# Hashed attention and Fourier mixing: the reciprocals of a head pair copied in two parts, and sums of weight quarters placed behind the newest mask or tally

## The chip, the cores and the metric

The kernel runs on one core of one Trainium2 chip. The metric is device time in microseconds (us), the median of several executions; before the change it is 1086.68 us (three runs, 1086.46 to 1087.05). The core has five engines that work side by side and wait for each other by semaphores: TensorE (PE, with its weight loads listed as PEld), VectorE (DVE), ScalarE (ACT), GpSimd (POOL) and SyncE (SP), which here only issues transfers.

## The reference

Two blocks follow each other. The first is attention over 4 batches of 8 heads, 768 positions and 64 numbers a head, in which a query sees only keys that fall in the same hash bucket:

```python
q_bits = (np.einsum('bhsd,dk->bhsk', q, proj) > 0).astype(np.int64)   # 6 bits; k likewise
mask = q_bucket[:, :, :, None] == k_bucket[:, :, None, :]
scores = scale * np.matmul(q, k.transpose(0, 1, 3, 2))
scores = np.where(mask, scores, -1000000000.0)
...
attn = attn / (np.sum(attn, axis=-1, keepdims=True) + 1e-09)
return np.matmul(attn, v).astype(np.float32)
```

The heads laid side by side make x (4 x 768 x 512). The second block mixes x by a Fourier transform and puts a normalised two-layer network behind it:

```python
mixed = np.real(np.fft.fft(np.fft.fft(x, axis=1), axis=2))
u = x + mixed
un = (u - mu) / np.sqrt(var + 1e-06)
ch = np.maximum(un @ w_ch1, 0.0) @ w_ch2      # 512 -> 2048 -> 512
return (u + ch).astype(np.float32)
```

## The kernel before, in words

**Pairs and chunks.** Two heads make a pair, so each batch has four pairs, n = 0 to 15 in all. A pair's 768 keys are taken in six chunks c of 128. For a chunk, `scores` (L884) multiplies keys and queries on PE into two banks (matmul `sc`, L905, one bank for each half of the queries); `weights` (L914) takes the exponential on ACT into a buffer `pk` (L916), of which there are two in turn; from pair 5 on, `weigh` (L920) multiplies by the mask of equal buckets on DVE (L930, one instruction per head); `chunk` adds the result to a running tally `acc` on DVE (L1018), which becomes the denominator; and `values` (L936) multiplies by the values on PE (`oo`, L941). Because there are two `pk` buffers, the exponential of chunk c waits for the values and the tally of chunk c-2.

**The end of a pair.** `scale` (L947) is a generator, run in two steps. The first step moves the result to x on ACT, adds up the tally over the keys on PE (`sum`, L960), transposes the sums on DVE (L967) and takes reciprocals (L969, L970). The second step copies the reciprocals into place with eight small copies on ACT (L976, 32 x 12 numbers each), spreads them by a transpose on DVE (L977) and multiplies x by them (L981). The second step is called from the chunk loop of the next pair, at the next visit of that loop after the first step; `finish` (L987) does the first.

**Preparing a pair.** While pair n runs, `prepare` (L766) gets pair n+1 ready: the transposes of q and k on DVE (L779), the signs of the projections (matmul `bits`, L836; test on DVE, L840) and the bucket numbers (matmuls `qb` L850 and `kb` L860, moved out of the banks by copies or casts on DVE and ACT, L535 and L537).

**Mixing.** `fold` (L1083) and the rest of `mix` (L1116) make the Fourier transform: sums and differences on DVE, matmuls `cs` (L1133) and `A`, `B` (L1162), added to x on DVE (L1176). Then `mlp7` (L1383) does the network by a scheme of seven products in place of eight. Its first layer, `inner` (L1448), has products `h_p` (L1441) and their sums on ACT and DVE (L1463 to L1492); the second, `outer7` (L1295), has products `o` (L1320), each scaled and added to the result on DVE (L1332 and others) with some copied on ACT first (L1339, L1350, L1353). Banks for `sum`, `bits`, `cs`, `A`, `B`, `h_p`, `o` all come from one pool of two (`pt`, tiles of the pool `ps_1`); scores have their own two and values their own two.

**Weights.** During the mix of batch 0 the second layer's weights are converted from the form in which they arrive, and `weights2` (L1260) forms four sums of their quarters on DVE (L1286 to L1289), once for every two pieces converted, eight times in all.

**Order.** Batch 0's attention is under a hand-written order. From batch 1 on, the generator of the mix of batch b-1 is advanced inside the chunk loop of attention b, and a scheduler decides the order of each engine's queue from the order of the program, the dependencies and its own durations, with two helpers on top. `behind` (L877) ties an instruction to the newest scores or values matmul and raises its priority. `in_turn` (L684) ties what stands in it to the newest instructions on record in a table `done_by`, one for each engine; exponentials, masks, some copies and additions of the first layer and of the Fourier step enter themselves there:

```python
    def in_turn():
        with ExitStack() as st:
            for ins in done_by.values():
                st.enter_context(tc.issue_after(ins.ins))
            yield
```

Of the kernel before, what the change touches and what calls it, by code (L numbers as in the profile page):

```python
# [17 lines left out]
ALU = mybir.AluOpType  # L18
# [8 lines left out]
NPAIR = H // 2  # L27
# [458 lines left out]
def _main(  # L486
# [13 lines left out]
    nc = tc.nc  # L500
# [13 lines left out]
    def wt(shape, dtype, tag, name, bufs=2):  # L514
        return work.tile(shape, dtype, tag=tag, name=name, bufs=bufs)
# [4 lines left out]
    def pt(shape, name):  # L520

        turn[0] += 1
        if roomy[0] and turn[0] % 2:
            if turn[0] % 4 == 1:
                return ps_o.tile(shape, F32, tag="o", name=name)
            return ps_sc.tile(shape, F32, tag="sc", name=name)
        return ps_1.tile(shape, F32, tag="ps", name=name)
# [152 lines left out]
    ET = mybir.EngineType  # L680
    done_by = {}

    @contextmanager
# [6 lines that stand above are left out]
# [186 lines left out]
    @contextmanager  # L876
    def behind():  # L877

        with tc.issue_after(last[0].ins), tc.high_priority(offset=AHEAD):
            yield  # L880
# [55 lines left out]
    def values(n, c, pk, oos):  # L936

        for g in range(2):
            w = HALF + 1 - g
            for h in range(2):  # L940
                oo = nc.tensor.matmul(  # L941
                    oos[g][h * D : (h + 1) * D, 0:w], nat["v", n][:, (2 * c + h) * D : (2 * c + h + 1) * D],
                    pk[:, g, h, 0:w], start=(c == 0), stop=(c == NT - 1),
                )
        last[0] = oo

    def scale(n, oos, sums):  # L947


        x = xs[n // NPAIR][:, n % NPAIR]  # L950
        vs = wt([P, 1], F32, "vs", f"vs{n}")
        nc.scalar.copy(vs, oos[0][:, HALF : HALF + 1])
        halves = [x[:, g * HALF : (g + 1) * HALF] for g in range(2)]
        for g, xg in enumerate(halves):
            nc.scalar.activation(xg, oos[g][:, 0:HALF], AF.Identity, bias=vs)

        ps = pt([P, HALF], f"sum{n}")
        for i, part in enumerate(sums):
            for j in range(4):
                nc.tensor.matmul(  # L960
                    ps[32 * j : 32 * j + 32, :], ones, part[:, j // 2, j % 2],
                    start=(i == 0), stop=(i == len(sums) - 1),
                )


        rt = wt([P, S], F32, "rt", f"rt{n}", 1)
        nc.vector.transpose(rt[:, 0:HALF], ps)  # L967
        rc = wt([P, HALF // 32], F32, "rc", f"rc{n}")
        nc.vector.tensor_scalar(rc, rt[:, 0:HALF:32], S * EPS, None, op0=ALU.add)  # L969
        nc.vector.reciprocal(rc, rc)  # L970
        yield
        rr = wt([P, 2, HALF // 32], F32, "rr", f"rr{n}")
        for g in range(2):
            for i in range(4):
                j = 2 * g + i // 2
                nc.scalar.copy(rr[32 * i : 32 * i + 32, g], rc[32 * j : 32 * j + 32])  # L976
        nc.vector.transpose(  # L977
            rt.rearrange("p (j i) -> p j i", i=32),
            rr.rearrange("p g j -> p (g j)")[:, :, None].broadcast_to([P, S // 32, 32]),
        )  # L980
        nc.vector.tensor_tensor(x, x, rt, op=ALU.mult)  # L981

    def attention(b):
        xs[b] = wt([P, NPAIR, S], F32, "x", f"x{b}")
        pending, scales = [], []

        def finish():  # L987
            n, c, pk, oos, sums = pending.pop(0)
            with behind() if n >= NPAIR and t is not None else nullcontext():
                values(n, c, pk, oos)  # L990
            if c == NT - 1:
                scales.append(scale(n, oos, sums))
                next(scales[-1])

        for t in range(NPAIR):
            n = NPAIR * b + t
            half = fold(b, 0) if t == NPAIR - 1 else iter(())
            if 1 < n + 1 < NPAIR * B:
                load(n + 1)
            ahead = prepare(n + 1) if n + 1 < NPAIR * B else iter(())  # L1000
            oos = [ps_o.tile([P, 512], F32, tag="o", name=f"oo{n}_{g}") for g in range(2)]
            acc = wt([P, 2, 2, HALF], F32, "acc", f"acc{n}", 1)
            first = None
            def chunk(c, pss):

                nonlocal first
                pk = weigh(n, c, pss)
                new = pk[:, :, :, 0:HALF]
                sums = [acc]
                if c == 0:  # L1010
                    first = new
                elif c == NT - 1 and b == 0:

                    sums.append(new)
                else:

                    for g in (0, 1) if b == 0 else (slice(0, 2),):
                        nc.vector.tensor_tensor(  # L1018
                            acc[:, g], (first if c == 1 else acc)[:, g], new[:, g],
                            op=ALU.add,  # L1020
                        )
                return n, c, pk, oos, sums

            for c in range(NT):
                if n < TWO:
                    new = chunk(c, scores(n, c))

                    for sc in scales:
                        next(sc, None)
                    scales.clear()  # L1030
                    while pending:
                        finish()
                    for sc in scales if b else ():
                        next(sc, None)
                    pending.append(new)
                elif c % 2 == 0:
                    pss = scores(n, c)
                    if len(pending) > 1:
                        finish()
                    new = [chunk(c, pss)]  # L1040
                    if pending:
                        finish()
                    new.append(chunk(c + 1, scores(n, c + 1, True)))
                    for sc in scales:
                        next(sc, None)
                    scales.clear()
                    pending += new
                if c > (3 if b == 1 else 2):
                    next(half, None)
                if c > 0:  # L1050
                    next(ahead, None)
                yield
        t = None
        while pending:
            finish()
        for sc in scales:
            next(sc, None)
# [202 lines left out]
    def weights2():  # L1260

        slices = []
        for half in range(2):
            for r in range(HF // 2):
                for hi, first in ((0, B11), (1, B21)):
                    c = half * HF // 2 + r + hi * HF

                    step = 1 if hi else T1 - B11
                    dst = w2f[:, 0 : 7 * QB].rearrange("p (i r n) -> p i r n", i=7, n=HD)
                    slices.append(  # L1270
                        (dst[:, first : first + step + 1 : step, r],
                         moe_w_ch2[c * P : (c + 1) * P, :])
                    )
        arrival = Arrival(slices, [zt2[:, i] for i in range(2)], NDC * DFF // WC, nc.gpsimd)
        for half in range(2):
            if half == 0:
                for i in range(arrival.depth):
                    arrival.fetch(i)
                yield
            for i in range(HF):  # L1280
                with in_turn():
                    arrival.convert(half * HF + i)
                yield
                if i % 2:
                    b11, b21, b22, t4, t1, t2, t3 = (q[:, i // 2] for q in right7)
                    nc.vector.tensor_tensor(t3, b22, t1, op=ALU.subtract)  # L1286
                    nc.vector.tensor_tensor(t1, t1, b11, op=ALU.subtract)
                    nc.vector.tensor_tensor(t2, b22, t1, op=ALU.subtract)
                    nc.vector.tensor_tensor(t4, b21, t2, op=ALU.subtract)  # L1289
            for i in range(7):  # L1290
                nc.sync.dma_start(bd[half, i], right7[i])
            if half == 0:
                yield
# [256 lines left out]
    for b in range(B):  # L1550
# [42 lines left out]
        if b == 0:  # L1593
            zt2 = wt([P, 3, 2 * WC], F32, "z", "zraw2", 1)
            arrival2 = weights2()
            other = after(NT, other, islice(arrival2, HF + 2))
# [47 lines left out]
```

## Time and profile before

| | |
|---|---|
| median of three runs | 1086.68 us |
| profiled execution | 1086.83 us, of which span 1085.0 us |
| granted TensorE clock | 0.995 of full speed |
| PE busy | 1034.9 us (95%) |
| DVE busy | 789.9 us (73%) |
| ACT busy | 498.4 us (46%) |
| POOL busy | 58.3 us (5%) |
| L976 copies | 128, median 198 ns |
| L1286 to L1289 sums | 32, about 0.42 us each |

The span runs from the first to the last instruction of the profiled execution. Rows of the timeline give start, duration, engine, line, operation, output and inputs, shapes, the number of instructions in the row, and in square brackets the idle time before it with what ended it. The chain of waits follows the work that ended last back to the start and shows its shares by engine. Lines are those of the kernel before.

### The profile page before, as it was taken

To read this page: it belongs to the slowest core of one execution; us is meant where nothing else is said; L and a number is where in the kernel's file an instruction comes from. 1 tells how busy PE (TensorE), PEld (TensorE's weight loads), DVE (VectorE), ACT (ScalarE), POOL (GpSimd) and SP (SyncE) were. 2 spreads that over 40 slices of the span, in tenths; PEclk is the share of its full clock that TensorE was granted. 3 is DMA by queue.
4 is the path that set the end of the run, shared out by engine and by line. 5 is a ranking of instruction groups with operands and counts; after the bars stand their busy time and mean duration, and the time that the engine had idled before them with its cause. 6 is when DMAs were issued, how large, how long until landed. Compare 5 with 4: busy or idle time off the path is not lost.

```text
span 1085.0 us, 14130 instructions
## 1 busy us (share of the span) xinstructions
PE 1034.9 (95%) x4933; PEld 633.1 (58%) x4933; DVE 789.9 (73%) x1336; ACT 498.4 (46%) x1055; POOL 58.3 (5%) x132
## 2 busy tenths in 40 slices
PE   7989898999999999999999999999999999999997
PEld 3333364547644675545664576645675579768676
DVE  5899969887699978685948776876865875644353
ACT  6988554762277233545335424354315522340430
POOL 0000000002000020010000020001000002100000
PEclk9999999999999999999999999999999999999999
DMA  8663452380056260223062233213033205122401
GB/s 214 190 142 76 97 144 54 121 243 1 22 133 229 71 205 15 59 68 83 11 190 72 60 97 126 44 44 91 17 100 100 73 20 175 58 80 85 129 20 42
DMA packets 175710, 103.13 MB, mean 95 GB/s; under 512 B 129552, under 2 KB 162960, under 8 KB 175632
## 3 DMA queue, kind: packets, MB, share of 16 engines
q1 hardware_dynamic: 169840, 88.65, 30.3%
q0 software_dynamic: 4224, 13.11, 3.9%
q8 instruction: 41, 0.67, 0.3%
q10 hardware_dynamic: 1568, 0.39, 0.2%
q14 instruction: 37, 0.30, 0.1%
HBM read 81.14 MB, written 20.97 MB: 94 GB/s over the span
## 4 chain that ended last, share of the span: by engine, by line
PE 64%; DVE 24%; ACT 6%; issue 3%; SPq 1%; DMA 1%; DVEq 0%; ACTq 0%
PE o L1320 24%; PE h_p L1441 19%; PE oo L941 7%; PE sc L905 6%; DVE pk L930 5%; DVE acc L1018 5%; PE cs L1133 2%; PE A L1162 1%; ACT pk L916 1%; ACT rr L976 1%; PE B L1162 1%; DMA kn<-in_k_dram 1%; SPq L576 1%; DVE w L643 1%; DVE qt L779 1%
## 5 line engine op out<-in xcount | busy, mean ns | idle before, releaser
L1320 PE MATMUL o<-w,h 128*128 128x256 f32 x1152 | 258.8, 381 | 2.4 <-ACT tq L1339 0.9
L1320 PEld LDWEIGHTS o<-w,h 128*128 128x128 f32 x1152 | 216.7, 190 | 42.9 <-issue 4.3
L916 ACT ACTIVATE pk<-sc 128x768 f32<-128x768 f32 x192 | 147.3, 808 | 98.2 <-PE sc L905 32.9
L1441 PE MATMUL h_p<-x,w 128*128 128x384 f32 x448 | 162.3, 492 | 0.1
L905 PE MATMUL sc<-qt,kt 64*128 64x384 f32 x768 | 154.8, 506 | 3.6 <-ACT pk L916 3.3
L930 DVE SCALAR_TENSOR_TENSOR pk<-qb,kb,pk 128x768 f32<-128x768 bf16 x132 | 128.9, 1011 | 33.4 <-ACT pk L916 33.1
L941 PE MATMUL oo<-pk,vn 128*64 128x385 f32 (+1 forms) x768 | 148.1, 497 | 4.0 <-DVE pk L930 3.4
L1441 PEld LDWEIGHTS h_p<-x,w 128*128 128x128 f32 x448 | 82.6, 190 | 64.2 <-issue 7.7
L1018 DVE TENSOR_TENSOR acc<-acc,pk 128x1536 f32<-128x1536 f32 (+1 forms) x72 | 105.8, 1484 | 5.8 <-ACT pk L916 5.1
L1441 PE MATMUL h_p<-w 128*128 128x384 f32 x288 | 106.4, 492 | 3.5 <-ACT w L1478 2.3
L941 PEld LDWEIGHTS oo<-pk,vn 128*64 128x64 f32 x768 | 50.8, 136 | 91.6 <-issue 74.2
L905 PEld LDWEIGHTS sc<-qt,kt 64*128 64x128 f32 x768 | 66.9, 188 | 55.0 <-issue 19.3
L1441 PEld LDWEIGHTS h_p<-w 128*128 128x128 f32 x288 | 53.0, 190 | 45.5 <-ACT w L1490 5.1
L1332 DVE SCALAR_TENSOR_TENSOR w<-o,rs,w 128x256 f32<-128x256 f32 x56 | 26.7, 479 | 42.6 <-PE o L1320 42.6
L1350 ACT COPY tq<-o 128x256 f32<-128x256 f32 x24 | 8.9, 372 | 102.6 <-PE o L1320 102.6
L1320 PE MATMUL o<-w 128*128 128x256 f32 x176 | 42.1, 382 | 1.0 <-DVE w L1332 1.0
L1474 DVE TENSOR_TENSOR h<-h 128x384 f32<-128x384 f32 x32 | 17.7, 553 | 30.3 <-ACT h L1473 30.3
L1320 PEld LDWEIGHTS o<-w 128*128 128x128 f32 x176 | 33.0, 190 | 7.7 <-DVE w L1332 2.0
L1467 DVE TENSOR_TENSOR h<-h 128x384 f32<-128x384 f32 x32 | 17.7, 553 | 26.6 <-ACT h L1466 26.6
L1071 POOL DMA_DIRECT2D out_dram<-w x30 | 16.4, 548 | 368.1 <-ACT tq L1350 146.2
L1366 DVE TENSOR_TENSOR tq<-tq,o 128x256 f32<-128x256 f32 x24 | 10.0, 418 | 35.0 <-PE o L1320 35.0
L1339 ACT COPY tq<-o 128x256 f32<-128x256 f32 x24 | 8.8, 368 | 54.0 <-PE o L1320 53.9
(170 smaller groups left out, 1332.9 us busy)
## 6 DMA issues: line engine op xcount, KB each, us to landing
w<-ad SPq DMA_DIRECT2D x168, 128.0 KB, 2.0
w<-bd SPq DMA_DIRECT2D x42, 512.0 KB, 4.5
zraw<-in_moe_w_ch_dram POOLq DMA_DIRECT2D x16, 512.0 KB, 4.2
bd<-w SPq DMA_DIRECT2D x14, 512.0 KB, 3.6
vn<-in_v_dram SPq DMA_DIRECT2D x32, 192.0 KB, 3.5
qn<-in_q_dram SPq DMA_DIRECT2D x120, 48.0 KB, 2.4
kn<-in_k_dram SPq DMA_DIRECT2D x60, 96.0 KB, 3.1
zraw<-in_moe_w_ch_dram SPq DMA_DIRECT2D x8, 512.0 KB, 6.8
```

Of the source, the lines that this page charges most:

```text
L905: last[0] = nc.tensor.matmul(ps[:, h, 0:HALF], kt[rows, ks], qt[rows, qs], start=kb is not None, stop=True,)
L916: done_by[ET.Activation] = nc.scalar.activation(pk[:, g, :, 0:HALF], ps[:, :, 0:HALF], AF.Exp, scale=SCALE)
L930: done_by[ET.DVE] = nc.vector.scalar_tensor_tensor(w, qb[:, h].rearrange("p (g s) -> p g s", g=2), kb[:, h, c : c + 1], w, op0=ALU.is_equa ...
L941: oo = nc.tensor.matmul(oos[g][h * D : (h + 1) * D, 0:w], nat["v", n][:, (2 * c + h) * D : (2 * c + h + 1) * D], pk[:, g, h, 0:w], start=( ...
L1018: nc.vector.tensor_tensor(acc[:, g], (first if c == 1 else acc)[:, g], new[:, g], op=ALU.add,)
L1133: nc.tensor.matmul(ps[:, pc + 2 * lo : pc + 2 * hi - 1 : 2], z[:, cp, pc, par, t * P : (t + 1) * P], ch[:, cp, pc, lo:hi], start=(cp == 0) ...
L1162: nc.tensor.matmul(ps[:, cols], F[:, par, k, t, j * P : (j + 1) * P], sq[:, t, k, cols], start=(t == 0), stop=(t == 1),)
L1320: nc.tensor.matmul(ps, a[:, r], right7[i][:, r], start=start and r == 0, stop=r == HF // 2 - 1, skip_group_check=not start,)
L1332: nc.vector.scalar_tensor_tensor(t[:, cols], src, r, t[:, cols], op0=ALU.mult, op1=ALU.add)
L1441: nc.tensor.matmul(ps, left[:, k], right[i][:, k], start=start and k == 0, stop=k == 1, skip_group_check=not start,)
L1467: done_by[ET.DVE] = nc.vector.tensor_tensor(c21, c12, c21, op=ALU.add)
L1474: done_by[ET.DVE] = nc.vector.tensor_tensor(c22, c21, c22, op=ALU.add)
```

## The change

Three things change, and no instruction is added or taken away. First, `scale` gets `t`, which is None at the end of a batch's attention. For pairs from 4 on whose scale runs inside the batch (pairs 4, 5, 6, 8, 9, 10, 12, 13 and 14) the eight copies go in two groups of four, each group tied by `in_turn`, and between the groups the generator gives up control, so that the second group, the transpose L977 and the multiplication L981 are issued one visit of the chunk loop later. The loop that advances the unfinished scales keeps those that are not done. Second, the tally addition L1018 enters itself in `done_by`. Third, the four sums of weight quarters stand in `in_turn`.

```diff
-    def scale(n, oos, sums):
+    def scale(n, oos, sums, t):
...
         rr = wt([P, 2, HALF // 32], F32, "rr", f"rr{n}")
         for g in range(2):
-            for i in range(4):
-                j = 2 * g + i // 2
-                nc.scalar.copy(rr[32 * i : 32 * i + 32, g], rc[32 * j : 32 * j + 32])
+            with in_turn() if n >= NPAIR and t is not None else nullcontext():
+                for i in range(4):
+                    j = 2 * g + i // 2
+                    nc.scalar.copy(
+                        rr[32 * i : 32 * i + 32, g], rc[32 * j : 32 * j + 32]
+                    )
+            if n >= NPAIR and t is not None and g == 0:
+                yield
...
-                scales.append(scale(n, oos, sums))
+                scales.append(scale(n, oos, sums, t))
...
-                        nc.vector.tensor_tensor(
+                        done_by[ET.DVE] = nc.vector.tensor_tensor(
                             acc[:, g], (first if c == 1 else acc)[:, g], new[:, g],
...
-                    for sc in scales:
-                        next(sc, None)
-                    scales.clear()
+                    scales[:] = [sc for sc in scales if next(sc, True) is None]
...
-                    nc.vector.tensor_tensor(t3, b22, t1, op=ALU.subtract)
-                    nc.vector.tensor_tensor(t1, t1, b11, op=ALU.subtract)
-                    nc.vector.tensor_tensor(t2, b22, t1, op=ALU.subtract)
-                    nc.vector.tensor_tensor(t4, b21, t2, op=ALU.subtract)
+                    with in_turn():
+                        nc.vector.tensor_tensor(t3, b22, t1, op=ALU.subtract)
+                        nc.vector.tensor_tensor(t1, t1, b11, op=ALU.subtract)
+                        nc.vector.tensor_tensor(t2, b22, t1, op=ALU.subtract)
+                        nc.vector.tensor_tensor(t4, b21, t2, op=ALU.subtract)
```

## The prediction

> **What bounds the kernel.** I read the busy shares first, then the chain of waits, then the timeline where TensorE (PE) stands still.
>
> ```profile
> PE 1034.9 (95%) x4933; PEld 633.1 (58%) x4933; DVE 789.9 (73%) x1336; ACT 498.4 (46%) x1055; POOL 58.3 (5%) x132
> PE 64%; DVE 24%; ACT 6%; issue 3%; SPq 1%; DMA 1%; DVEq 0%; ACTq 0%
> ```
>
> PE is idle for 1085.0 - 1034.9 = 50 us. Listing PE's idle intervals from the timeline, about 24 lie before 140 us (loading, and the first batch in its hand-written order), 8 in the tail, and some 24 between 150 and 930 us, in pieces of 0.2 to 1.7 us. The change reaches only these last ones. 24% of the chain is DVE, so DVE is not always cover: in the busy time by windows it has 25.35 of 27.0 us at 163 to 190, and 25.52, 26.09 and 27.11 of 27.0, 27.0 and 28.0 from 298 to 380. Against that:
>
> ```profile
> core 0: us, PE busy (x) PEld busy (x) DVE busy (x) ACT busy (x) POOL busy (x), PEclk, DMA share, GB/s
> 776.00:812.00 36.00, 36.00 (x181) 25.20 (x180) 27.07 (x37) 8.43 (x15) 0.00 (x0) 1.00 0.19 62
> ```
>
> Here, in pair 14, PE loses nothing and DVE has 9 us to spare. An order that piles DVE work ahead of PE here can only lose.
>
> Each kind of stall the change touches has a place in the timeline (start, duration, engine, instruction, [idle before, releaser]). Quarter sums ahead of a transpose that frees a bank for PE:
>
> ```profile
> 168.97 0.42 DVE L1286 TENSOR_TENSOR w<-w 128x256 f32<-128x256 f32 x1
> ...
> 170.69 0.58 DVE L967 STREAM_TRANSPOSE rt<-sum 128x384 f32<-128x384 f32 x1
> ...
> 171.33 0.92 PE L1162 MATMUL B<-sq,F 128*128 128x193 f32 x4 [0.69 <-DVE rt L967]
> ```
>
> Eight reciprocal copies ahead of a copy that PE waits for, in batch 2 (batch 3 repeats it at 716.79 with 1.14):
>
> ```profile
> 456.59 1.65 ACT L976 COPY rr<-rc 32x12 f32<-32x12 f32 x8
> ...
> 458.26 0.48 ACT L1478 COPY w<-h_p 128x384 f32<-128x384 f32 x1
> ...
> 458.80 1.56 PE L1441 MATMUL h_p<-w 128*128 128x384 f32 x4 [1.13 <-ACT w L1478]
> ```
>
> And the DVE queue just ahead of pair 11's bits, where PE waits for an addition that stands behind a tally:
>
> ```profile
> 541.10 1.72 DVE L1018 TENSOR_TENSOR acc<-acc,pk 128x1536 f32<-128x1536 f32 x1
> 542.73 0.47 DVE L1332 SCALAR_TENSOR_TENSOR w<-o,rs,w 128x256 f32<-128x256 f32 x1
> ...
> 543.26 4.58 PE L1320 MATMUL o<-w,h 128*128 128x256 f32 x20 [0.57 <-DVE w L1332]
> 547.78 0.52 PE L836 MATMUL bits<-qt,pj 128*32 128x384 f32 x2
> ```
>
> [...] The rows at 456.59 and 541.10 agree: a copy waits 1.65 us behind eight small ones, an addition 1.72 behind a tally. The forecast goes by it: every instruction waits for what is ahead of it, ready or not. [...] what follows the split here is DVE's (27.11 of 28.0 us in one window). [...]
>
> **The change.** It adds and removes nothing: 128 copies of 0.198 us, 32 quarter sums of 0.42, all transfers remain. What changes is order. I built both programs and laid their queues side by side, engine by engine. PE keeps its order to the first h_p of batch 0's mix (about 163 us), and has the same again in the last MLP half. Between, the scheduler, given other constraints, also moves chunks of scores and values among the MLP products, and moves DVE (457 differing lines), ACT (230), SP (58) and POOL (4) with them. SP's moved loads are w, qn and kn fetches with room (SP waits, not the users), POOL's four are stores; I cost these at 0 to 0.5. I go place by place through the new order, with durations from the trace: exp pair 1.5, mask pair 1.9, tally 1.72, transpose L977 0.9 when pipelined, multiply L981 0.9, score pair 1.5, values of a chunk 1.4, product o 1.74, product h_p 1.45. Plus is gain.
>
> 1. *168 to 217, pair 4's scale.* The four sums (4 x 0.42) leave the front of the L967 transpose: its gap of 0.69 goes, as does one of 0.87 at 198.64. But DVE stays the limit to 245 us and the same sums return behind the masks. Between 0 and 2; I take **+0.6**.
> 2. *235 to 250, pair 5's scale.* Four of eight copies (0.8) leave the front of an exp for which PE waited 1.03, then 0.93 on its mask. The mask now stands ahead of L977. Between -0.2 and 1.9; **+0.8**.
> 3. *305 to 375.* The gap of 1.67 at 321.01 shrinks by 0.8, but DVE is 97% busy afterwards. **0**, within 1.
> 4. *374 to 402, start of pair 8.* Its first scores move ahead among the o products; their exp stands behind pair 7's eight copies (not split at its end) which wait for the reciprocal: a PE stall of 1.65 to 2.4, against 0.95 + 0.27 removed. Between -2 and 0; **-1.0**.
> 5. *450 to 500 and 708 to 758.* The L1478 copy has four copies ahead instead of eight: 1.13 falls to 0.3. Chunks 4 and 5 move into h_3, so gaps of 0.69 and 0.57 go: +2.1. The kb matmuls of pairs 10 and 14 now wait for a 0.95 cast of qb queued behind two masks and a tally (1.9 + 1.7): about -1.1. Between -0.5 and 2 each; **+1.0 twice**.
> 6. *518 to 550, pair 10, and 776 to 810, pair 14.* This carries the forecast. New PE order from the scores of chunk 2, at S: scores, values of 0 and 1, scores, two o products, scores, values of 2 and 3, scores, o_0_2_3, three quarters of o_0_2_0, bits. That is 4 x 1.5 + 2 x 2.8 + 3 x 1.74 + 1.3 = 18.1, so PE wants bits at S + 18.1. Their bank is freed by the DVE addition of o_0_2_3 (L1332). DVE starts chunk 2's masks at S + 3.95 (exp waits for values: 2.4; exp pair 1.55, as at 521.11 and 523.12). Ahead of the addition, then: masks 1.9, tally 1.72, masks 1.9, L977 0.9, tally 1.72, L981 0.9, five MLP instructions 2.3, masks of chunk 4 with one between 2.3, an addition 0.45, tally 1.72, half of chunk 5's masks 0.95. With the addition's 0.47 that is 17.2, less about 0.45 of overlap of neighbours: 16.75. So S + 20.7, a stall of 2.5. Next, o_0_2_4 waits for the bits' bank, freed by L840 behind a mask and, in batch 2, an L779 transpose (1.1), in batch 3 a mask and a tally (1.9). The 0.57 at 543.26 goes. Sum -3.0 in batch 2, between -4 and 0.5; **-3.0**. In batch 3, -4.4, less 0.2 for the overlap of neighbours; between -5 and 0; **-4.2**.
> 7. *597 to 625, pair 11.* kb of pair 12 waits for its cast as in 5: -1.25. Values of one chunk are split and lose overlap, -0.35; gaps of 0.60 and 0.20 may go. Between -1.6 and 0.8; **-1.0**.
>
> Sum: 0.6 + 0.8 + 0 - 1.0 + 2.0 - 3.0 - 4.2 - 1.0 = **-5.8**. The profiled execution took 1086.83 (span 1085.0, 1.83 around it), so 1092.6; the median of the runs is 1086.68, 0.15 lower: **1092.5**.
>
> The cover of what I cost at nothing: the second part of the copies, one visit later, hides behind PE's chunk, for x is not read before the next mix. If it were late, L977 and L981 would be late with it: that is the pile-up in 6.
>
> **Rivals.** A difference under 0.2% (2.2 us) is about what a measurement can't tell from no change.
>
> - *A, the forecast: DVE's pile-up holds the bits and kb.* For: no idle PE in 776 to 812 that could absorb it. Against: my 16.75 is 18% over the room of 14.2; an error of two instructions takes most of the stall away. Its own range, with the stalls of 6 within about 3 us in sum and the others within their bounds: 1089 to 1097. Chance 0.60.
> - *B, faster: DVE drains in time.* It needs the addition at S + 18.1 in place of S + 20.7, and the cast before kb. It decides at 14.2 us of DVE work ahead of bits instead of 16.75: if L977, L981 or one tally falls behind the bits. Then 6 gives only +0.6, 5 gives +2.1 twice, 7 nothing: 0.6 + 0.8 - 1.0 + 4.2 + 0.6 = 5.2 gained, 1081.5. For: the places 2 and 5 are seen in the trace and the split surely shortens them. Against: it needs the order that I read to be harmless. Chance 0.28.
> - *C, no difference.* Half of the stalls in 5 to 7 are covered (about 5.5 us of their 11): 1086.7, within 2.2. Chance 0.12.
> - *The change does nothing:* where a pair's copies stand is set by the newest exponential, and the order would be as before. Excluded by the order: over 450 DVE lines differ.
>
> The range takes in A and C and B down to its middle: 1082 to 1097, leaving out 0.14 below and some 0.06 above. Chances: faster 0.28, same 0.12, slower 0.60.
>
> **What would show it.** For 6: bits of pairs 11 and 15 with about 2.5 idle, released by L1332, and o next with 1 to 2, released by L840. For 5 and 7: kb with about 1.1, released by L535; L1478 with 0.3. For 1: no gap at L1162 released by L967. For 4: a score of pair 8 released by an exp behind eight copies. I am wrong if bits and kb start without idle time; then B holds. If they stall as said and the time still falls, gains in 1 to 3 were larger than I allowed.

## The result, and the profile after

The changed kernel takes 1095.71 us (median of five runs, 1093.09 to 1097.48) against 1086.68 before; the ratio is 1.0084, 95% interval 1.0072 to 1.0095. It is slower, by 9.0 us where 5.8 were forecast, and inside the range. The profiled execution took 1093.09 (span 1091.1), 6.3 above that of before. From the copies on, lines lie 1 to 5 higher in the new numbering: the tally L1018 is L1023, the copies are L977, the transpose and the multiplication L982 and L986, the additions of L1332 now L1336, products o L1324 and h_p L1445.

The page of the changed kernel, busy times and chain:

```profile
PE 1036.1 (95%) x4933; PEld 634.8 (58%) x4933; DVE 786.0 (72%) x1336; ACT 499.8 (46%) x1055; POOL 59.1 (5%) x132
PE 62%; DVE 25%; ACT 5%; issue 3%; SPq 2%; DMA 1%; DVEq 0%; ACTq 0%
```

Same work, 1.2 us more PE time, and idle time up from 50.1 to 55.0 us. Averages do not say where. A lag table does. Each pair ends with one group of `sum` matmuls (L960), and both traces have these groups in the same order. The start of a pair's sum in the new trace less its start in the old one (the lag) tells how far the new kernel is behind, or ahead where it is negative; the step from one pair to the next is what that stretch cost.

| up to the sum of pair | before, us | after, us | lag | step | places of the forecast | forecast |
|---|---|---|---|---|---|---|
| 4 | 168.61 | 167.53 | -1.08 | | none: the same order | |
| 5 | 233.35 | 231.25 | -2.10 | -1.02 | 1 | -0.6 |
| 6 | 304.43 | 300.99 | -3.44 | -1.34 | 2 | -0.8 |
| 7 | 371.97 | 368.10 | -3.87 | -0.43 | 3 | 0 |
| 8 | 452.54 | 449.28 | -3.26 | +0.61 | 4 | +1.0 |
| 9 | 512.55 | 507.87 | -4.68 | -1.42 | 5 | -1.0 |
| 10 | 574.85 | 574.47 | -0.38 | +4.30 | 6 | +3.0 |
| 11 | 631.01 | 630.94 | -0.07 | +0.31 | 7 | +1.0 |
| 12 | 710.53 | 710.48 | -0.05 | +0.02 | none | |
| 13 | 770.54 | 769.07 | -1.47 | -1.42 | 5 | -1.0 |
| 14 | 832.00 | 836.94 | +4.94 | +6.41 | 6 | +4.2 |
| 15 | 886.20 | 892.59 | +6.39 | +1.45 | none | |

The first row is hardly the change's: PE has its old order almost to its end, and the profiles of the ten versions tried below lie between -0.99 and +0.52 there. The two stretches that end with the sums of pairs 10 and 14 lose 10.7 us; everything else together gains. In the new timeline, this is what stands ahead of the bits of pair 11 (start, duration, engine, instruction, idle time before it and what ended it):

```profile
542.14 1.75 DVE L1023 TENSOR_TENSOR acc<-acc,pk 128x1536 f32<-128x1536 f32 x1
543.81 1.02 DVE L930 SCALAR_TENSOR_TENSOR pk<-qb,kb,pk 128x768 f32<-128x768 bf16 x1
544.74 0.48 DVE L1336 SCALAR_TENSOR_TENSOR u<-o,rs,u 128x256 f32<-128x256 f32 x1
545.27 0.52 PE L836 MATMUL bits<-qt,pj 128*32 128x384 f32 x2 [2.51 <-DVE u L1336]
...
806.47 0.75 PE L836 MATMUL bits<-qt,pj 128*32 128x384 f32 x2 [2.51 <-DVE u L1336]
...
809.66 3.78 PE L1324 MATMUL o<-w 128*128 128x256 f32 x8 [0.61 <-DVE bt L840]
```

Both bits wait 2.51 us for the addition behind a tally and a mask, and the next product waits again for L840. In pair 10 the scores of chunk 2 began at 524.39, and the addition ended at 545.22, 20.8 later; the forecast had 20.7. But look at the durations in the last two rows, of pair 14's stretch: the bits take 0.75 where those at 545.27 took 0.52, and eight o matmuls take 3.78 where eight took 1.89 in the trace of before. The busy time by windows (column before the last two: the granted PE clock) says why:

```profile
core 0: us, PE busy (x) PEld busy (x) DVE busy (x) ACT busy (x) POOL busy (x), PEclk, DMA share, GB/s
540.00:560.00 20.00, 16.71 (x75) 11.67 (x74) 15.04 (x23) 2.70 (x6) 0.00 (x0) 0.91 0.51 167
800.00:820.00 20.00, 16.87 (x69) 11.49 (x66) 12.28 (x18) 3.06 (x5) 0.00 (x0) 0.83 0.38 128
```

The rows show a mean of 0.91 and 0.83 because PE ran at half rate for a part of each window, behind the waits: 0.09 x 20 = 1.8 us lost in pair 10, 0.17 x 20 = 3.4 in pair 14. Both windows have 1.00 in the trace of before. That was in no step of the forecast.

The wait that was feared at kb, and the copy that was to come earlier:

```profile
454.70 0.91 PE L1445 MATMUL h_p<-w 128*128 128x384 f32 x2 [0.30 <-ACT w L1482]
...
489.43 1.76 DVE L1023 TENSOR_TENSOR acc<-acc,pk 128x1536 f32<-128x1536 f32 x1
491.11 0.95 DVE L535 CAST qb<-qb 128x768 bf16<-128x768 f32 x1
...
492.11 0.24 PE L860 MATMUL kb<-pw,bt 32*128 32x2 bf16 x6 [0.27 <-DVE qb L535]
```

h_p waits 0.30 in place of 1.13, as forecast. kb waits 0.27, not 1.1: the two masks (487.45 to 489.40) were done before the qb matmuls were, so only the tally stood ahead of the cast, and two h_p matmuls filled most of that.

The start of pair 8, and a place that the forecast did not name, in pair 15:

```profile
372.59 1.67 ACT L977 COPY rr<-rc 32x12 f32<-32x12 f32 x8
...
375.15 0.92 PE L905 MATMUL sc<-qt,kt 64*128 64x384 f32 x4 [1.59 <-ACT pk L916]
...
880.56 1.75 DVE L1023 TENSOR_TENSOR acc<-acc,pk 128x1536 f32<-128x1536 f32 x1
882.23 0.87 DVE L1336 SCALAR_TENSOR_TENSOR w<-o,rs,w 128x256 f32<-128x256 f32 x2
882.76 1.99 PE L1324 MATMUL o<-w 128*128 128x256 f32 x8 [2.30 <-DVE w L1336]
```

The first two rows show pair 7's eight copies, behind which the exp that the scores wait for stands (L916); this is the wait of place 4. In the last three PE's order is the old one; what moved is pair 14's multiplication. In the two traces, first before and then after:

```profile
839.08 0.95 DVE L981 TENSOR_TENSOR x<-x,rt 128x768 f32<-128x768 f32 x1
840.88 0.95 DVE L1093 TENSOR_TENSOR ef<-x 128x768 f32<-128x768 f32 x1
...
868.04 1.95 DVE L930 SCALAR_TENSOR_TENSOR pk<-qb,kb,pk 128x768 f32<-128x768 bf16 x2
```

```profile
861.53 0.95 DVE L986 TENSOR_TENSOR x<-x,rt 128x768 f32<-128x768 f32 x1
...
863.33 0.95 DVE L1096 TENSOR_TENSOR ef<-x 128x768 f32<-128x768 f32 x1
...
868.15 0.96 DVE L1096 TENSOR_TENSOR ef<-x 128x768 f32<-128x768 f32 x1
...
874.44 1.02 DVE L930 SCALAR_TENSOR_TENSOR pk<-qb,kb,pk 128x768 f32<-128x768 bf16 x1
```

The first fold of batch 3 (L1093, now L1096) reads x of pairs 12 and 14 while pair 15 still runs. With the multiplication one visit later, the fold moves from 840 to 863 and later, in front of the masks of chunk 4. These then begin 1.7 us behind the start of their neighbours on PE (scores at 872.73), where before they began 0.25 ahead of them (868.29), and the wait of 0.34 at 876.36 became 2.30.

### The profile page after: what moved, and what is told of

It reads as the page before. It is cut to its first block, busy times and chain, and to the rows that moved or that the text cites. A ratio compares the mean times of both kernels' runs of the same rounds, so it can differ in the third digit from the quotient of the medians.

```text
span 1091.1 us, 14120 instructions
## 1 busy us (share of the span) xinstructions
PE 1036.1 (95%) x4933; PEld 634.8 (58%) x4933; DVE 786.0 (72%) x1336; ACT 499.8 (46%) x1055; POOL 59.1 (5%) x132
## 4 chain that ended last, share of the span: by engine, by line
PE 62%; DVE 25%; ACT 5%; issue 3%; SPq 2%; DMA 1%; DVEq 0%; ACTq 0%
PE o L1324 24%; PE h_p L1445 19%; PE oo L941 6%; DVE pk L930 6%; DVE acc L1023 6%; PE sc L905 5%; PE cs L1136 2%; ACT pk L916 2%; SPq L576 2%; PE A L1165 1%; PE B L1165 1%; DMA kn<-in_k_dram 1%; DVE x L1179 1%; DVE w L643 1%; PE sum L960 1%
## 5 line engine op out<-in xcount | busy, mean ns | idle before, releaser
L1324 PE MATMUL o<-w,h 128*128 128x256 f32 x1152 | 259.7, 382 | 0.8 <-DVE w L1336 0.6
L1324 PEld LDWEIGHTS o<-w,h 128*128 128x128 f32 x1152 | 217.1, 190 | 42.0 <-issue 5.9
L916 ACT ACTIVATE pk<-sc 128x768 f32<-128x768 f32 x192 | 147.4, 808 | 86.7 <-PE sc L905 30.6
L1445 PE MATMUL h_p<-x,w 128*128 128x384 f32 x448 | 163.4, 493 | 2.8 <-ACT h L1467 1.9
L1445 PEld LDWEIGHTS h_p<-x,w 128*128 128x128 f32 x448 | 81.7, 190 | 67.5 <-ACT h L1467 6.1
L1023 DVE TENSOR_TENSOR acc<-acc,pk 128x1536 f32<-128x1536 f32 (+1 forms) x72 | 106.0, 1486 | 5.8 <-ACT pk L916 5.1
L1445 PE MATMUL h_p<-w 128*128 128x384 f32 x288 | 106.0, 489 | 0.6 <-ACT w L1482 0.6
L1445 PEld LDWEIGHTS h_p<-w 128*128 128x128 f32 x288 | 53.4, 190 | 40.0 <-ACT w L1482 2.0
L1336 DVE SCALAR_TENSOR_TENSOR w<-o,rs,w 128x256 f32<-128x256 f32 x56 | 26.8, 481 | 50.9 <-PE o L1324 50.9
L1324 PE MATMUL o<-w 128*128 128x256 f32 x176 | 45.7, 406 | 3.9 <-DVE w L1336 2.5
L1324 PEld LDWEIGHTS o<-w 128*128 128x128 f32 x176 | 34.9, 203 | 12.6 <-DVE w L1336 4.8
```

Source lines behind the costliest of these rows:

```text
L916: done_by[ET.Activation] = nc.scalar.activation(pk[:, g, :, 0:HALF], ps[:, :, 0:HALF], AF.Exp, scale=SCALE)
L1023: done_by[ET.DVE] = nc.vector.tensor_tensor(acc[:, g], (first if c == 1 else acc)[:, g], new[:, g], op=ALU.add,)
L1324: nc.tensor.matmul(ps, a[:, r], right7[i][:, r], start=start and r == 0, stop=r == HF // 2 - 1, skip_group_check=not start,)
L1336: nc.vector.scalar_tensor_tensor(t[:, cols], src, r, t[:, cols], op0=ALU.mult, op1=ALU.add)
L1445: nc.tensor.matmul(ps, left[:, k], right[i][:, k], start=start and k == 0, stop=k == 1, skip_group_check=not start,)
```

## The experiments

Theory: the time is lost where VectorE holds up the bits of pairs 11 and 15, and nowhere else to speak of. Rivals: the loss is spread over all nine pairs (kb, split value products); it comes from the sums or the tally; or from the second part coming a visit later at all. The order helps here: from sum to sum, PE's queue in most such variants is that of the kernel before or that of the changed one, so parts can be undone one pair at a time. Each ratio below is to runs of the kernel before taken beside those of the version, whose medians lie between 1087.01 and 1087.16 us.

**Five pairs.** The condition on the tie and on the pause becomes

```diff
-            with in_turn() if n >= NPAIR and t is not None else nullcontext():
+            with in_turn() if n in (4, 5, 6, 8, 12) and t is not None else nullcontext():
...
-            if n >= NPAIR and t is not None and g == 0:
+            if n in (4, 5, 6, 8, 12) and t is not None and g == 0:
```

> As the changed kernel, but only pairs 4, 5, 6, 8 and 12 copy in two parts; 9, 10, 13 and 14 copy as before. The order of PE then equals the changed kernel's up to the end of pair 9 and again in pair 13, and the order of before elsewhere. Theory (the loss sits where pairs 10 and 14 hold the bits behind VectorE): the gains stay, the losses go; by the lag between the two traces from sum to sum that is -1.0 -1.3 -0.4 +0.6 -1.4 -1.4 = -5.0, so about 1081.7 us, no idle over 1 us at bits, clock 0.995. Rival (the loss is spread: kb casts, split value products, copies held back everywhere): 1086 to 1090.

Measured: 1082.12 us, ratio to before 0.9952 (0.9936 to 0.9969): faster than both kernels, and within 0.5 us of what the steps of the table add up to. Its timeline at pair 11's bits:

```profile
543.17 0.52 PE L836 MATMUL bits<-qt,pj 128*32 128x384 f32 x2
...
544.92 1.89 PE L1324 MATMUL o<-w 128*128 128x256 f32 x8
```

There is no wait, and PE runs at full rate. A loss spread over all pairs would not leave five of them with the whole gain.

**Pairs 10 and 14 as well** (`n not in (9, 13)` in the same condition).

> As the first of this set, but pairs 10 and 14 copy in two parts as well, only 9 and 13 as before. PE's order is the same as in the first; VectorE's differs in pairs 11 and 15 alone. Theory (the idle 2.30 us at o in pair 15 comes from the multiplication and transpose of pair 14 landing there): that idle time is back, 1.4 to 1.8 us slower than the first, about 1083.3 us. Rival (it came from the late arrival out of the stall at the bits): as fast as the first.

Measured: 1085.89 us, 0.9991 (0.9983 to 1.0). The wait in pair 15 is back (2.31), with no stall at the bits ahead of it. So it comes from pair 14's second part; the rival (late arrival) falls. The time is 3.8 us above the five pairs, not 1.4 to 1.8. The trace shows two reasons: 0.95 us more from sum 10 to sum 11 (57.07 against 56.12, with waits of 1.92 and 0.89 that end at 611.81 and 614.26), and half rate again, in

```profile
873.54 3.68 PE L1324 MATMUL o<-w 128*128 128x256 f32 x8 [2.31 <-DVE w L1336]
```

where the changed kernel's profile, after the same wait of 2.30, has 1.99.

**Only pairs 9 and 13** (`n in (9, 13)`; sums and tally as changed).

> Sums and tally as changed, but only pairs 9 and 13 copy in two parts. The order at both bits is that of the changed kernel. Theory: idle 2.5 us at the bits of 11 and 15, PE at half rate behind them (eight o matmuls in 3.5 us instead of 1.9), 4.3 and 6.4 us lost; with the gains of pairs 6 to 8 of about 1.2 that is 1095 us, from 1093 to 1097, clock near 0.99. Rival (the half rate was an accident of the execution): idle 2.5, but full rate behind it and clock 0.995, about 1091 us. Rival (all nine splits share the loss): 1087 to 1089.

Measured: 1097.65 us, 1.0096 (1.0074 to 1.0117). Two of nine pairs bring more than the whole loss, and the half rate is there again, at both places; the rows are those of the first:

```profile
547.73 0.52 PE L836 MATMUL bits<-qt,pj 128*32 128x384 f32 x2 [2.52 <-DVE u L1336]
...
549.98 3.78 PE L1324 MATMUL o<-w 128*128 128x256 f32 x8 [0.74 <-DVE bt L840]
```

From sum 9 to sum 10 it needs 67.98 us where before has 62.30, from 13 to 14 67.98 against 61.46.

**Two parts without the tie.** `with in_turn() ...` around the copies is taken away, the pause stays in all nine pairs.

> As the changed kernel with all nine pairs in two parts one visit apart, but without the tie behind the newest exponential; sums and tally as changed. In the order, bits of 11 and 15 now stand ahead of the scores of chunk 4 and the addition that frees their bank ahead of the masks of chunk 4. Theory (not the pause but the queue ahead of that addition costs the time): no idle over 1 us at bits, about 1082 us, to 1084 if pair 15's stall stays. Rival (the second part one visit later is itself the cost, since transpose and multiplication fall into a full VectorE): still 1090 or more.

Measured: 1083.47 us, 0.9965 (0.9954 to 0.9976). The pause alone is not the cost. In the timeline, the bits now go first, and the scores of chunk 4 behind them:

```profile
538.75 0.52 PE L836 MATMUL bits<-qt,pj 128*32 128x384 f32 x2
...
539.53 1.56 PE L905 MATMUL sc<-qt,kt 64*128 64x384 f32 x8
```

So the cost is the order that the scheduler chose under pause and tie together. The tie without the pause was not run; the scheduler leaves the bits of both pairs where they were before with it. The wait in pair 15 is gone too (54.19 us from sum 14 to sum 15, as before).

**Shorter tallies.** Does the wait's length set the half rate? In the version with only 9 and 13, the tally of chunk 2 of pairs 10 and 14 gets fewer columns (W), and the other columns are left out of the sum. This leaves all orders as they are and takes VectorE time from the queue ahead of the bits:

```diff
-                            acc[:, g], (first if c == 1 else acc)[:, g], new[:, g],
+                            *(u[:, g, :, 0 : W if n in (10, 14) and c == 2 else HALF]
+                              for u in (acc, first if c == 1 else acc, new)),
```

W = 192, 320 and then 48 of 384. These kernels have one line more, so L1337 and L1325 are the L1336 and L1324 of the others.

> The version with only pairs 9 and 13 in two parts (1097.65 us), with the tally of chunk 2 of pairs 10 and 14 over half its columns (the rest of that tally is left out). The order of every engine stays the same; VectorE has 0.85 us less ahead of each bits. Theory (idle time over some 2.3 us is what halves PE's rate): idle at bits 2.52 to 1.66, no half rate behind it, so 2 x 0.85 and 1.7 to 3.4 more at each place come back: 1089.5 to 1092.5 us, clock 0.995 or more. Rival (the half rate belongs to the place, its mix of matmuls or several short waits together): only 1.7 comes back, 1096 us, clock 0.992.

> The same with the tally of chunk 2 of pairs 10 and 14 over 320 of 384 columns (the rest left out): VectorE has 0.28 us less ahead of each bits, idle 2.52 to 2.24. Below the 2.31 after which the half rate was seen, above the 1.92 after which it was not. If it stays: 1097 us. If it goes: 1090.5 to 1093 us. If it comes in some executions only: in between, with a wide spread.

> As the version with the tally over half its columns, but over 48 of 384 columns in chunk 2 of pairs 10 and 14 (the rest left out). The order stays. VectorE has about 1.45 us less ahead of the bits than in the version with full tallies: idle at both bits about 1.1. Behind the bits, idle 0.77 in pair 11 and 1.7 in pair 15 stay. If several short waits close together add up: at the bits of 11 (1.9 in all) full rate comes back, at 15 (2.8 in all) half rate stays for one spell of 1.7 lost; 1091.5 to 1092.5 us. If each place halves the rate whatever the idle time: 1093.5. If a single wait over 1.5 us is needed: half rate at 15 alone, behind the 1.7.

Measured: 1094.71 us for 192 (1.0064, 1.0052 to 1.0076), 1097.60 for 320 (1.0086, 1.0072 to 1.0101), 1094.26 for 48 (1.0066, 1.0054 to 1.0079). With 192 columns:

```profile
547.51 0.52 PE L836 MATMUL bits<-qt,pj 128*32 128x384 f32 x2 [1.72 <-DVE u L1337]
...
549.77 3.54 PE L1325 MATMUL o<-w 128*128 128x256 f32 x8 [0.77 <-DVE bt L840]
```

The wait fell by the 0.8 us that VectorE was spared, which confirms that its queue sets it. The half rate stayed: my idea that one wait of over 2.3 us is needed falls. It was shorter (0.91 in both 20 us windows, against 0.83 in both with all columns and with 320), which is 1.6 us less lost by the clock at each place. In all, the two stretches took 2.1 and 1.1 us less. The second gained less because the wait behind pair 15's bits grew from 0.82 to 1.70: the bits now ran at full rate and were done sooner, while VectorE's queue ahead of L840 stayed. With 48 columns nothing more came:

```profile
534.97 1.95 DVE L930 SCALAR_TENSOR_TENSOR pk<-qb,kb,pk 128x768 f32<-128x768 bf16 x2 [0.50 <-ACT pk L916]
...
548.26 0.52 PE L836 MATMUL bits<-qt,pj 128*32 128x384 f32 x2 [1.71 <-DVE u L1337]
...
375.88 1.49 PE L905 MATMUL sc<-qt,kt 64*128 64x384 f32 x4 [1.59 <-ACT pk L916]
```

I had not seen that the mask of chunk 3 then waits for its exponential, so the wait at the bits is 1.71 and not 1.1, and this run could not decide between its three outcomes. By accident its last row is of use: here the score matmuls behind a wait of 1.59 took 1.49 in place of 0.92, at half rate; the same wait of 1.59 left the rate alone (0.92) in the other eight profiles that have it.

**The sums alone** (nothing but `in_turn` around L1286 to L1289).

> The kernel before with the quarter sums alone placed behind the newest mask (no tally on record, copies as before). PE's order is the one of the version with only pairs 9 and 13 to the end of pair 8, then that of before. From that version's lags: 1.8 us faster, 1085.3 us. Rival (the gain up to 370 us belongs to the copies of pairs 4 to 6): no difference, 1087.

Measured: 1086.19 us, 0.9992 (0.9986 to 0.9999). The trace has the 1.7 us from sum 4 to sum 8 (282.20 against 283.93), the medians differ by 0.8.

**The copies alone** (no sums, tally not on record).

> The changed kernel without the sums and without the tally on record: the nine pairs in two parts alone. PE's order is that of before in pairs 5, 8, 12 and 15 and that of the changed kernel in 6, 9, 10, 11, 13 and 14. By the lags: -1.3 (6) -1.4 (9) +4.3 (10) +0.3 (11) -1.4 (13) +6.4 (14), +1.5 to 3.5 (15): 8.4 to 10.4 slower, about 1096 us. Rival (the sums are what delayed the later pairs): 1082 to 1085.

Measured: 1095.77 us, 1.0077 (1.0064 to 1.0089), with 2.52 and 2.51 idle at the two bits and 2.30 in pair 15. The copies bring the loss without the sums and without the tally on record.

**Five pairs, copies alone.**

> The five pairs (4, 5, 6, 8, 12) in two parts without the sums and without the tally on record. PE's order is that of before in pairs 5 and 8 and that of the version with five pairs elsewhere but for pair 7. If the gain comes from the copies: by the lags of the run with copies alone 1082.3, as fast as with the sums (1082.12). If the sums carry a share that the copies do not also give: 1083 to 1084.

Measured: 1082.40 us, 0.9956 (0.9943 to 0.9969). The gain of the five pairs needs neither the sums nor the tally. The tally on record alone was not run: with it, the scheduler gives every engine the same order as in the kernel before.

## Why the prediction was right

- **Place 6** carried the loss, as said: bits of 11 and 15 with 2.51 idle (forecast 2.5), released by L1332's successor L1336, the addition at S + 20.8 (20.7). The second waits, forecast as 1.1 and 1.9, were 0.77 and 0.61 in the changed kernel; where PE took pair 15's bits at full rate, in the run with the copies alone, the second was 1.70. The term that was mis-sized is that for what follows: I counted idle time only, and PE lost another 1.8 and 3.4 us at half rate. +4.30 and +6.41 were measured for +3.0 and +4.2; in the profile, 2.51 + 0.77 + 1.8 less the old gap of 0.57 makes 4.5, and 2.51 + 0.61 + 3.4 makes 6.5.
- **Places 1 and 2** gained 2.36 us where 1.4 were taken, within the bounds. The idle 1.03 ahead of the scores at 241.62 fell to 0.19 (at 238.08 in the new trace); the 0.69 at L1162 went, though 0.72 came at 171.91, where PE now waits for L1179, the Fourier step's addition.
- **Place 3** gave 0.43 for 0, **place 4** cost 0.61 for 1.0, by the mechanism named (1.59 idle behind eight copies).
- **Place 5** gained 1.42 twice, for 1.0, as h_p's wait fell to 0.30 as forecast and kb waited 0.27 instead of 1.1. The step that failed is "queued behind two masks and a tally": I counted what is ahead in the queue, not what of it is still to do when the cast's input is ready.
- **Place 7** cost 0.31 for 1.0, for the same reason: kb of pair 12 waits 0.27.
- **Pair 15** was missed: +1.45 in this profile. The step that failed is the cover: "x is not read before the next mix". The fold inside pair 15 reads it, and VectorE's order changed there though PE's did not. The run without pairs 9 and 13, against the five pairs, shows that pair 14's second part brings it.
- **What was luck.** The profile's steps from pair 5 on add up to +7.5 where the places added up to +5.8. They come so close because misses cancel: place 6 and pair 15 cost 3.5 and 1.45 us more than the forecast had, and the other places together 3.3 less. Two slips in its working did not matter: by its own figures the stall of place 6 is 20.7 - 18.1 = 2.6, and PE's idle time ahead of 140 us is 18 us, not 24 (its three parts would make 56 of 50).
- **From the profile to the median.** The profiled execution is the fastest of the five; the others are 1.8 to 4.4 us slower and have clocks of 0.991 and 0.988 where it has 0.993. More half-rate spells in those executions would do that, as behind the wait of 2.30 in pair 15 (2.31 in the version without pairs 9 and 13), which half rate followed in one of the three profiles that have it; those executions have no trace, so this is argued.
- Rival B (VectorE drains in time) is not what happened, yet its gain is real: the five pairs, which keep the old order at both bits, reach 1082.12 against the 1081.5 that B was given.

## What to carry to other kernels

Where the change is one of order, go through the new order of every engine, place by place, and ask of each wait which queue holds its releaser and how many microseconds of that queue are unfinished when the releaser's own input is ready; adding up durations put the addition ahead of the bits within 0.1 us here, while the waits for kb, where only the queue's length was counted, came out 0.8 too long. An engine at 72% on average, as VectorE here, can be the one that decides where three or four large instructions stand together, so a delay that is good in one stage has to be looked at again in each later stage in which it is used. And price a wait of TensorE above its length: some of the waits of 1.59 to 2.52 us here were followed by matmuls at half rate, which cost 1.7 or 3.4 us more.

## What the runs showed of the hardware

In the six kernels with the pile-up, PE ran at half rate at all twelve bits places, behind waits of 1.71 to 2.52. Behind single waits of 2.30 or 2.31 it did so in one of three profiles, behind a wait of 1.59 in one of nine. In the changed kernel's profile the granted clock was 0.50 in these two stretches (columns as in the table by windows above):

```profile
547.25:550.60 3.35, 3.07 (x7) 2.52 (x8) 3.35 (x5) 0.00 (x0) 0.00 (x0) 0.50 0.57 176
806.65:813.45 6.80, 6.19 (x19) 3.58 (x12) 3.91 (x5) 0.00 (x0) 0.00 (x0) 0.50 0.23 77
```

Half of 3.4 and of 6.8 us is the 1.7 and 3.4 us that the clock cost at the two places.

The length of a wait did not tell by itself whether half rate followed. Here are the 20 us around the wait in pair 15, in the changed kernel (2.30) and in the version without pairs 9 and 13 (2.31):

```profile
870.00:890.00 20.00, 17.70 (x86) 12.54 (x86) 15.53 (x25) 4.69 (x9) 0.63 (x1) 1.00 0.03 9
...
870.00:890.00 20.00, 17.69 (x80) 12.23 (x79) 12.21 (x24) 3.92 (x14) 2.26 (x4) 0.91 0.08 27
```

PE was busy for 17.70 and 17.69 us, and the granted clock was 1.00 in one and 0.91 in the other. Behind the wait, eight o matmuls took 1.99 us in the first and 3.68 in the second. What sets such waits apart stays open.
